# Cluster attention and two feed-forward layers on one core: preparation of the second and third pair of heads placed earlier, with a third buffer of queries and keys

## The chip, the cores and the metric

The kernel runs on one core of a Trainium2 chip, as one program. The metric is the device time of one execution in microseconds (us). Three executions of the kernel before gave 790.48, 790.6 and 793.39 us, with a median of 790.6 us.

## The reference

What is computed, cut to what matters (2 batches, 8 heads, 768 positions, 64 features a head, 16 centroids a head):

```python
def _attn_ref(q, k, v, centroids):
    q_n = q / (norm(q) + 1e-06); k_n = k / (norm(k) + 1e-06); c_n = centroids / (norm(centroids) + 1e-06)
    q_assign = np.argmax(np.einsum('bhsd,hcd->bhsc', q_n, c_n), axis=-1)
    k_assign = np.argmax(np.einsum('bhsd,hcd->bhsc', k_n, c_n), axis=-1)
    mask = q_assign[:, :, :, None] == k_assign[:, :, None, :]
    scores = np.where(mask, scale * q @ k.T, -1000000000.0)
    attn = softmax(scores)
    return attn @ v

x = attention output as [1536, 512]
h = np.maximum(x @ w_in, 0.0);  x = (h * h) @ w_out
h = x @ w_in2;                  out = (h * sigmoid(1.702 * h)) @ w_out2
```

A query sees only the keys of its own cluster. Inputs and result are float32, except that the weights come as float64 words.

## The kernel before

The work of attention goes by pairs of heads: eight pairs `p` (four a batch), two heads a pair. Scores are computed tile by tile: `scores(s)` is 128 queries of one head against all 768 keys, 96 tiles in all, and the two heads of a pair alternate, so that twelve tiles make a pair. A tile goes through `scores` (TensorE, L517 and L520, four matmuls into `ps_s`), `peak` (VectorE, L526, the row's extreme), `exponents` (ScalarE, L534), `turn` (TensorE, L542, twelve transposes for two tiles), `keep` (copies out of PSUM by VectorE and ScalarE, L550), and after six tiles `values` (TensorE, L560). There are two `ps_s` buffers, so that the matmuls of a tile wait for the exponentials of the tile two before. All other PSUM tiles (`ps_aff`, `ps_back`, `ps_oh`, `ps_p`, `ps_v`, `ps_r`) share four banks.

Before its first tile, a pair is prepared by `prep(p)`:

- `load` brings queries and keys (`raw_q`, `raw_k`) by the SP queue, L266. `q_high`, `k_high` (L357, L347) round them on ScalarE, `q_low`, `k_low` (L362, L352) subtract on GpSimd (POOL), each with a DMA that doubles the rounded half.
- `square` (L371) squares queries and keys, on ScalarE (L369) for the first two pairs and on POOL from the third on. `aff` (L378, L381) multiplies queries and keys by the centroids and sums the squares, in two halves of 384 positions; `aff_out` (L387) copies this to `cst`. These are the "products" below.
- `back` (L395) transposes `cst`, `back_out` (L405) copies it to `ar`; `root` (L409, POOL) and `inv_norm` (L415, L416, VectorE) make inverse norms, `scale` (L428, POOL), `most` (L436, VectorE), `less` (L439, POOL), `first`, `least`, `one_hot` (L443, L447, L454, VectorE) find the nearest centroid as a one-hot row.
- `mask` (L461) transposes the one-hot rows, `mask_out` copies them out of PSUM (L470 and L472 for the first pair, L477 for the others), and for the later pairs four DMAs (L482) put them below the queries and keys, where they enter L520 as 16 more rows of the contraction.

The order is written out by hand. Every step has a key, a number; all steps of the kernel are sorted by it, and each engine carries its own out strictly in that order. The tables FIRST (first pair), SECOND (second) and PAIR (all others) hold the keys of `prep`, counted from 12 times the pair; GROUP holds those of two tiles, two key units apart, from -1 on. So `aff` of the second pair, with -60.03 in SECOND, has key -48.03, and that of the third pair, with -15.15 in PAIR, has key 24 - 15.15 = 8.85. After the last pair the two feed-forward layers follow, matmuls of 128x512 (L656, L695), the weights converted by VectorE, ScalarE and POOL beside them (L191 to L213).

Of the kernel before, what the change touches and what calls it, by code (L numbers as in the profile page):

```python
# [8 lines left out]
F32 = mybir.dt.float32  # L9
# [7 lines left out]
P = 128  # L17
# [15 lines left out]
PAIR = dict(  # L33
    load_q=-20.601, load_k=-20.501, load_v=-5.2, square=(-16.9, -16.5),
    aff=(-15.15, -15.1), aff_out=(-14.95, -14.8), back=(-13.15, -13.1), back_out=(-12.95, -12.8),
    k_high=(-13.4, -6.9), k_low=(-12.95, -6.3), q_high=(-12.6, -10.7), q_low=(-12.2, -8.9),
    root=-12.7, inv_norm=-9.95, scale=-9.9, most=-8.98, less=-8.95, first=-6.98,
    least=-6.95, one_hot=-6.0, mask=(-5.15, -5.1), mask_out=(-4.95, -4.8),
)
# [5 lines left out]
FIRST = dict(  # L45
    load_v=-46.0, centres=-51.127, windows=-51.026, warm=(-51.2, -51.02, -48.752),
    square=(-49.995, -49.985), q_high=(-49.99, -49.98), k_high=(-48.1, -49.97),
    q_low=(-49.9, -49.8), k_low=(-47.95, -49.7),
    aff=(-49.195, -49.095), aff_out=(-49.145, -49.045), back=(-48.995, -48.895), back_out=(-48.95, -48.85),
    root=(-48.8, -48.7), inv_norm=-48.6, scale=-48.5, most=-48.4, less=-48.3, first=-48.117, least=-48.1,  # L50
    one_hot=-48.0, mask=(-47.9, -47.7), mask_out=(-47.859, -47.659, -47.559, -47.459), table=-48.107,
)
SECOND = dict(
    load_q=-62.0, load_k=-62.0, load_v=-1.143, square=(-60.05, -60.04), aff=(-60.03, -60.02), aff_out=(-59.44, -59.43),
    back=(-12.6, -12.59), back_out=(-12.5, -12.4), root=-12.35, inv_norm=-10.2, scale=-10.15, most=-8.25,
    less=-8.2, first=-6.98, least=-6.97, one_hot=-5.9, mask=(-3.15, -3.1), mask_out=(-2.95, -2.8),
    q_high=(-11.3, -5.4), q_low=(-10.1, -5.3), k_high=(-4.9, -3.4), k_low=(-4.8, -3.3),
)


# [5 lines left out]
def cluster_attention_then_two_ffns(  # L66
# [17 lines left out]
    nc = tc.nc  # L84
    B, H, D, S = q_t.shape
# [16 lines left out]
    scale = 1.0 / float(D) ** 0.5  # L102
# [6 lines left out]
    ROOM = {F32R: 96 * KB, F32: 110 * KB}  # L109
# [51 lines left out]
    g_at = [14 * KB + 6 * KB * m for m in range(MF)]  # L161
    g_t = [view(a, [NC, CH]) for a in g_at]
    tmp, o_p = Places(4 * KB, 10 * KB), Places(0, g_at[0])
    words_at = (0, 10 * KB)
    places = Places(g_at[0], g_at[15])


    def weight(layer, which, m):
# [7 lines left out]
    def w_stages(layer, which, m, place):  # L176
# [35 lines left out]
        def low():  # L212
            nc.gpsimd.tensor_tensor(out=halves[:, 1, :], in0=x[0].bitcast(F32), in1=halves[:, 0, :].bitcast(F32),  # L213
                                    op=ALU.subtract)

        return load, [magnitude, clamp, shift, join_low, join_high, high, low]


    with tc.manual_schedule():
        with ExitStack() as actx:  # L220
# [7 lines left out]
            one = places  # L228
# [5 lines left out]

            def early():

                for nm in ("raw_q", "raw_k", "sq"):
                    for _ in range(2):
                        places.tile([P, S], F32, tag=nm, bufs=2)
                places.tile([P, S], F32, tag="cst")  # L240
                places.tile([P, NT, P], F32, tag="ar")
                places.tile([P, NT, 4, C], F32, tag="aff")

            early()
            KQ = D + C
            x_s, k1_s, q2_s, k2_s = [], [], [], []
# [10 lines left out]
            def load(p, nm):  # L257
                b, hp = PAIRS[p]
                heads = slice(2 * hp, 2 * hp + 2)
                if nm == "v":  # L260
                    t = two.tile([P, 2, NT, D], F32, tag="v", name="raw_v")
                    src = v[b, :, heads]
                else:
                    t = one.tile([P, S], F32, tag="raw_" + nm, name="raw_" + nm, bufs=2)
                    src = (q_t if nm == "q" else k_t)[b, heads].rearrange("h d s -> (h d) s")
                (nc.scalar if p == 0 and nm == "q" else nc.sync).dma_start(out=t, in_=src)  # L266
                raw[p, nm] = t

            cr = one.tile([P, D], F32, name="cr")
            nc.sync.dma_start(out=cr, in_=centroids)  # L270
            load(0, "q")
            load(0, "k")
            half = one.tile([P, NT, 2, 2], F32, name="half")
            nc.vector.memset(half, 0.5)
# [56 lines left out]
            def at(key, f, *args):  # L331
                events.append((key, len(events), lambda: f(*args)))
# [5 lines left out]
            def prep(p):  # L338
# [45 lines left out]
                def aff_out(u):  # L384
                    if u == 0:
                        h["cst"] = one.tile([P, S], F32, tag="cst", name="cst")
                    nc.scalar.copy(  # L387
                        out=h["cst"][:, u * HALF:(u + 1) * HALF], in_=h["aff", u][:, :HALF])

                USED = 6 * C + 2  # L390
# [91 lines left out]
                            nc.sync.dma_start(out=dst[D:D + C].bitcast(F32), in_=m[r * C:(r + 1) * C].bitcast(F32))  # L482

                def put(name, f, *args):
                    when = (FIRST, SECOND, PAIR)[min(p, 2)]
                    w = when[name]
                    start = NQ * p
                    if isinstance(w, tuple):
                        for x, key in enumerate(w):
                            at(start + key, f, x)  # L490
                    else:
                        at(start + w, f, *args)

                for nm in ("q", "k", "v") if p else ("v",):
                    put("load_" + nm, load, p, nm)
                for name, f in (("square", square), ("root", root), ("inv_norm", inv_norm), ("k_high", k_high), ("k_low", k_low),
                                ("q_high", q_high), ("q_low", q_low), ("aff", aff), ("aff_out", aff_out), ("back", back),
                                ("back_out", back_out), ("scale", scale_rows), ("most", most), ("less", less),
                                ("first", first), ("least", least), ("one_hot", one_hot), ("mask", mask),
                                ("mask_out", mask_out)):  # L500
                    put(name, f)
# [103 lines left out]
            for k in range(NG // 2):  # L605
# [4 lines left out]
                for b in range(3):  # L610
                    at(begin + GROUP["turn"][b], turn, k, b)
                    when = GROUP["keep"][b]
                    at(begin + (when if b < 2 else when[k % 2 == 0]), keep, k, b)
            for n in range(NH):
                when, begin = (LAST, 0.0) if n == NH - 1 else (HALVES, ORIGIN + 6 * n)
# [208 lines left out]
```

## Time and profile before

| what | value |
|---|---|
| median of three runs | 790.6 us (790.48 to 793.39) |
| the profiled execution's own time | 790.69 us |
| its span, first to last instruction | 788.9 us |
| what lies around the span | 1.79 us |
| mean granted TensorE clock | 0.993 |
| PE busy | 775.4 us, 98% of the span |
| VectorE (DVE) / ScalarE (ACT) / POOL busy | 457.6 / 418.2 / 203.3 us |
| chain that ended last, by engine | PE 88%, DVE 6%, ACT 3%, POOL 1%, issue 1% |
| chain, largest lines | L656 32%, L695 28%, L560 8%, L542 7%, L517 5%, L520 4% |

The busy rows say how long an engine had an instruction in it; the chain says which engine's work set the end, followed back from the last instruction. The span in 40 slices shows PE at nine tenths or more in all but the first two slices and the last, and a granted clock below nine tenths of full speed in one, the second. In the rows of the trace a start is in us from the span's start, and a bracket tells the idle time ahead of an instruction and who ended it.

### The profile page before, as it was taken

The numbers are of one execution on the slowest core, as the hardware profiler recorded it, in microseconds if no ns is written. First come the engines' busy times: TensorE is split into PE (matmuls) and PEld (weight loads), VectorE is DVE, ScalarE is ACT, GpSimd is POOL, SyncE is SP. The second block draws the span as 40 slices with busy tenths as digits, with TensorE's granted clock in tenths as the row PEclk, the third lists the DMA queues.
The fourth block names the chain that finished last, engine by engine and source line by source line (L and its number), as shares of the span: only waits on it lengthen the run. The fifth ranks groups of instructions, "written<-read, shape, count | busy, mean of one in ns | idle before, by whom it ended". The sixth has DMA issues, their size and how long they took to land.

```text
span 788.9 us, 10653 instructions
## 1 busy us (share of the span) xinstructions
PE 775.4 (98%) x3947; PEld 610.5 (77%) x3947; DVE 457.6 (58%) x813; ACT 418.2 (53%) x775; POOL 203.3 (26%) x158
## 2 busy tenths in 40 slices
PE   7899999999999999999999999999999999999998
PEld 5766767767776788888887888888888888788886
DVE  6657877868877444444477644445654557742222
ACT  6776887887876466666643433343333334432222
POOL 2564654654601122212122011101211112200000
PEclk9799999999999999999999999999999999999999
DMA  4232222222120122232233022101212112210002
GB/s 141 69 85 69 81 66 76 81 67 76 41 84 28 59 99 91 99 102 86 81 107 107 27 70 64 54 0 60 102 53 81 54 62 99 81 54 0 1 1 106
DMA packets 18195, 54.52 MB, mean 69 GB/s; under 512 B 2720, under 2 KB 2976, under 8 KB 18144
## 3 DMA queue, kind: packets, MB, share of 16 engines
q1 hardware_dynamic: 17856, 53.32, 21.4%
q8 instruction: 31, 0.51, 0.3%
q10 hardware_dynamic: 288, 0.52, 0.2%
q14 instruction: 20, 0.16, 0.1%
HBM read 43.02 MB, written 3.15 MB: 59 GB/s over the span
## 4 chain that ended last, share of the span: by engine, by line
PE 88%; DVE 6%; ACT 3%; issue 1%; POOL 1%; DMA 0%; ACTq 0%; DVEq 0%; POOLq 0%
PE bank L656 32%; PE bank L695 28%; PE ps_v L560 8%; PE ps_p L542 7%; PE ps_s L517 5%; PE ps_s L520 4%; PE ps_h L656 1%; DVE arena L683 1%; ACT arena L534 1%; PE ps_aff L378 1%; DVE arena L526 1%; PE ps_r L577 1%; DVE arena L206 1%; DVE arena L194 1%; DVE arena L202 1%
## 5 line engine op out<-in xcount | busy, mean ns | idle before, releaser
L695 PE MATMUL bank<-arena 128*128 128x512 f32 x1152 | 262.3, 389 | 0.6 <-DVE arena L683 0.6
L695 PEld LDWEIGHTS bank<-arena 128*128 128x128 f32 x1152 | 215.9, 188 | 46.7 <-DVE arena L683 2.0
L656 PE MATMUL bank<-arena 128*128 128x512 f32 x1104 | 250.6, 389 | 0.0
L656 PEld LDWEIGHTS bank<-arena 128*128 128x128 f32 x1104 | 207.2, 188 | 43.0
L213 POOL TENSOR_TENSOR arena<-arena,arena 128x512 fp32r<-128x512 f32 x64 | 82.7, 1292 | 368.0 <-ACT arena L210 307.6
L683 DVE TENSOR_TENSOR arena<-arena,arena 128x512 fp32r<-128x512 f32 x96 | 74.8, 781 | 106.4 <-ACT arena L679 105.1
L526 DVE TENSOR_SCALAR_CACHE_REDUCE arena<-ps_s 128x768 bf16<-128x768 f32 x96 | 91.7, 956 | 42.8 <-PE ps_s L520 35.1
L679 ACT CAST arena<-arena 128x512 fp32r<-128x512 f32 x96 | 59.1, 619 | 105.0 <-PE bank L695 105.0
L534 ACT ACTIVATE arena<-ps_s,arena 128x768 f32<-128x768 f32 x96 | 86.9, 906 | 38.9 <-DVE arena L526 38.5
L194 DVE TENSOR_SCALAR arena<-arena 128x512 f32<-128x512 f32 x64 | 38.4, 599 | 73.7 <-ACT arena L191 73.7
L210 ACT CAST arena<-arena 128x512 fp32r<-128x512 f32 x64 | 39.6, 618 | 64.9 <-DVE arena L206 64.9
L542 PE MATMUL ps_p<-arena 128*128 128x128 f32 x576 | 73.1, 278 | 0.0
L560 PE MATMUL ps_v<-arena 128*64 128x384 f32 x384 | 72.6, 501 | 0.0
L665 ACT ACTIVATE arena<-bank 128x512 f32<-128x512 f32 x48 | 28.7, 598 | 79.0 <-PE bank L656 79.0
L542 PEld LDWEIGHTS ps_p<-arena 128*128 128x128 f32 x576 | 67.9, 144 | 2.3 <-issue 0.6
L672 DVE TENSOR_TENSOR arena<-bank,arena 128x512 f32<-128x512 f32 x48 | 33.1, 690 | 58.0 <-ACT arena L665 58.0
L517 PE MATMUL ps_s<-arena 128*128 128x384 f32 x192 | 55.5, 370 | 4.1 <-ACT arena L534 3.9
L520 PE MATMUL ps_s<-arena 80*128 80x384 f32 x192 | 50.5, 344 | 0.6 <-ACT arena L472 0.5
L517 PEld LDWEIGHTS ps_s<-arena 128*128 128x128 f32 x192 | 31.8, 192 | 20.9 <-ACT arena L534 9.3
L550 DVE COPY arena<-ps_p 128x512 f32<-128x512 f32 x72 | 47.0, 677 | 0.8 <-PE ps_p L542 0.8
L202 DVE SCALAR_TENSOR_TENSOR arena<-arena 128x512 int32<-128x512 int32 x64 | 45.3, 708 | 2.0
L206 DVE SCALAR_TENSOR_TENSOR arena<-arena 128x512 int32<-128x512 int32 x64 | 44.2, 691 | 1.9
(93 smaller groups left out, 636.3 us busy)
## 6 DMA issues: line engine op xcount, KB each, us to landing
arena<-in_w_dram SPq DMA_DIRECT2D x64, 512.0 KB, 3.2
arena<-arena SPq DMA_DIRECT2D x32, 192.0 KB, 2.5
arena<-in_k_t_dram SPq DMA_DIRECT2D x8, 384.0 KB, 3.7
arena<-in_v_dram SPq DMA_DIRECT2D x8, 384.0 KB, 3.3
out_dram<-arena SPq DMA_DIRECT2D x11, 256.0 KB, 2.1
arena<-in_q_t_dram SPq DMA_DIRECT2D x7, 384.0 KB, 3.3
arena<-arena SPq DMA_DIRECT2D x28, 48.0 KB, 2.1
arena<-in_q_t_dram ACTq DMA_DIRECT2D x1, 384.0 KB, 3.5
```

The lines of the kernel that those rows point to most:

```text
L202: nc.vector.scalar_tensor_tensor(out=x[0], in0=words[:, :, 0], scalar=29, in1=x[0], op0=ALU.logical_shift_right, op1=ALU.bitwise_or)
L213: nc.gpsimd.tensor_tensor(out=halves[:, 1, :], in0=x[0].bitcast(F32), in1=halves[:, 0, :].bitcast(F32), op=ALU.subtract)
L517: nc.tensor.matmul(ps[:, n, :HALF], lhsT=x_s[i][:, t * P:(t + 1) * P], rhs=k1_s[i][:, n * HALF:(n + 1) * HALF], start=True, stop=False)
L520: nc.tensor.matmul(ps[:, n, :HALF], lhsT=q2_s[i][:, t * P:(t + 1) * P], rhs=k2_s[i][:, n * HALF:(n + 1) * HALF], start=False, stop=True)
L526: nc.vector.tensor_scalar(out=unused, in0=s_t[g][:, :, :HALF], scalar1=-scale, scalar2=None, op0=ALU.mult, op1=ALU.min, accum_out=m_t[g])
L534: nc.scalar.activation(out=p_t[g].rearrange("p (n f) -> p n f", n=2), in_=s_t.pop(g)[:, :, :HALF], func=AF.Exp, bias=m_t.pop(g), scale=sca ...
L542: nc.tensor.transpose(ps[:, x * P:(x + 1) * P], p_t[2 * k + j][:, t * P:(t + 1) * P], ident)
L560: nc.tensor.matmul(pv_t[n][j * D:(j + 1) * D, :HALF], lhsT=raw[n // 2, "v"][:, j, t, :], rhs=pt_t[n, j][:, t, :], start=(t == 0), stop=(t ...
L656: nc.tensor.matmul(ps, lhsT=w[:, a, kk * P:(kk + 1) * P], rhs=xf[:, b, kk, c * CH:(c + 1) * CH], start=(n == 0), stop=(n == 3 * KD - 1))
L679: nc.scalar.copy(out=half_of(m, c)[:, 0, :], in_=g_t[m][:, c, :])
L683: nc.vector.tensor_tensor(out=t[:, 1, :], in0=g_t[m][:, c, :], in1=t[:, 0, :].bitcast(F32), op=ALU.subtract)
L695: nc.tensor.matmul(ps, lhsT=lhsT, rhs=rhs, start=(m == 0 and e == 0), stop=(m == MF - 1 and e == 2))
```

## The change

It gives the third pair a table of its own, THIRD, and new keys to some steps of the second and third pair:

- Second pair: `aff_out` and `back` move between the first pair's `aff` and its first scores (keys -47.95 and -47.6; the first masks have -47.9 and -47.7). `back_out` and `root` keep their places behind the first pair's `mask_out`. `first` and `least` move behind the `peak` of the tiles 6 and 7 (tiles are counted from 0). The roundings of the second head move a little earlier.
- Third pair: queries and keys are loaded ahead of the first values' load, its squares come first on POOL after the first pair's `q_low`, `aff` stands behind the scores of tiles 0 and 1 (keys 0.85 and 0.9), `aff_out` goes from ScalarE to VectorE, `back` stands ahead of the scores of tile 10 (keys 8.9 and 8.92), `back_out` follows.
- `raw_q` and `raw_k` have three buffers in place of two; the memory of attention grows by 6 KB, to the end of its arena.

```diff
-    load_q=-62.0, load_k=-62.0, load_v=-1.143, square=(-60.05, -60.04), aff=(-60.03, -60.02), aff_out=(-59.44, -59.43),
-    back=(-12.6, -12.59), back_out=(-12.5, -12.4), root=-12.35, inv_norm=-10.2, scale=-10.15, most=-8.25,
-    less=-8.2, first=-6.98, least=-6.97, one_hot=-5.9, mask=(-3.15, -3.1), mask_out=(-2.95, -2.8),
-    q_high=(-11.3, -5.4), q_low=(-10.1, -5.3), k_high=(-4.9, -3.4), k_low=(-4.8, -3.3),
+    load_q=-62.0, load_k=-62.0, load_v=-1.143, square=(-60.05, -60.04), aff=(-60.03, -60.02), aff_out=(-59.95, -59.94),
+    back=(-59.6, -59.59), back_out=(-59.44, -59.43), root=-59.35, inv_norm=-10.2, scale=-10.15, most=-8.25,
+    less=-8.2, first=-6.2, least=-6.15, one_hot=-5.9, mask=(-3.15, -3.1), mask_out=(-2.95, -2.8),
+    q_high=(-11.3, -6.18), q_low=(-10.1, -6.1), k_high=(-5.45, -4.75), k_low=(-5.4, -4.7),
+)
+THIRD = dict(
+    PAIR, load_q=-71.9, load_k=-71.89, square=(-71.4, -71.39), aff=(-23.15, -23.1), aff_out=(-22.95, -22.9),
+    back=(-15.1, -15.08), back_out=(-14.75, -14.7),
 )
...
-    places = Places(g_at[0], g_at[15])
+    places = Places(g_at[0], ROOM[F32])
...
-                for nm in ("raw_q", "raw_k", "sq"):
-                    for _ in range(2):
-                        places.tile([P, S], F32, tag=nm, bufs=2)
+                for nm, n in (("raw_q", 3), ("raw_k", 3), ("sq", 2)):
+                    for _ in range(n):
+                        places.tile([P, S], F32, tag=nm, bufs=n)
...
-                    t = one.tile([P, S], F32, tag="raw_" + nm, name="raw_" + nm, bufs=2)
+                    t = one.tile([P, S], F32, tag="raw_" + nm, name="raw_" + nm, bufs=3)
...
-                    nc.scalar.copy(
+                    (nc.vector.tensor_copy if p == 2 else nc.scalar.copy)(
                         out=h["cst"][:, u * HALF:(u + 1) * HALF], in_=h["aff", u][:, :HALF])
...
-                    when = (FIRST, SECOND, PAIR)[min(p, 2)]
+                    when = (FIRST, SECOND, THIRD, PAIR)[min(p, 3)]
```

In the lists below, the lines of the changed kernel are four higher than those of the kernel before.

TensorE from the first masks (`ps_oh`) to the first transposes of exponentials (`ps_p`), first as before, then as changed:

```order
L461 MATMUL ps_oh<-arena_58 128x128 x6
L517 MATMUL ps_s<-arena_58 128x384 x2
L520 MATMUL ps_s<-arena_58 128x384 x2
L517 MATMUL ps_s<-arena_58 128x384 x2
L520 MATMUL ps_s<-arena_58 128x384 x2
L395 MATMUL ps_back<-arena_59 128x98 x6
L517 MATMUL ps_s<-arena_58 128x384 x2
```

```order
L465 MATMUL ps_oh<-arena_58 128x128 x6
L399 MATMUL ps_back<-arena_59 128x98 x6
L521 MATMUL ps_s<-arena_58 128x384 x2
L524 MATMUL ps_s<-arena_58 128x384 x2
L521 MATMUL ps_s<-arena_58 128x384 x2
L524 MATMUL ps_s<-arena_58 128x384 x2
L382 MATMUL ps_aff<-arena_59 32x384 x2
L385 MATMUL ps_aff<-arena_59 32x384 x2
L382 MATMUL ps_aff<-arena_59 32x384 x2
L385 MATMUL ps_aff<-arena_59 32x384 x2
L521 MATMUL ps_s<-arena_58 128x384 x2
```

The six transposes of the second pair went ahead of the scores of tiles 0 and 1, and the eight products of the third pair came in behind them.

POOL from the first pair's `q_low` on, as before and as changed (`arena` is the memory that holds all tiles; 128x768 are squares, 128x24 is `root`):

```order
L362 TENSOR_TENSOR arena_58<-arena_59,arena_58 64x768
L409 TENSOR_TENSOR arena_59<-arena_59 128x24
L428 TENSOR_TENSOR arena_59<-arena_59 128x384
L362 TENSOR_TENSOR arena_58<-arena_59,arena_58 64x768
L439 TENSOR_TENSOR arena_59<-arena_59 128x384
L571 COPY arena_59<-arena_59 128x384
L362 TENSOR_TENSOR arena_58<-arena_59,arena_58 64x768
L371 TENSOR_TENSOR arena_59<-arena_59 128x768
```

```order
L366 TENSOR_TENSOR arena_58<-arena_59,arena_58 64x768
L375 TENSOR_TENSOR arena_59<-arena_59 128x768 x2
L413 TENSOR_TENSOR arena_59<-arena_59 128x24
L432 TENSOR_TENSOR arena_59<-arena_59 128x384
L366 TENSOR_TENSOR arena_58<-arena_59,arena_58 64x768
L443 TENSOR_TENSOR arena_59<-arena_59 128x384
L366 TENSOR_TENSOR arena_58<-arena_59,arena_58 64x768
```

Both squares of the third pair went ahead of the second pair's `root`.

VectorE around the tiles 4 to 7, as before and as changed (128x768 is `peak`, 128x4x128 a copy of transposed exponentials):

```order
L550 COPY arena_59<-ps_p 128x4x128 x2
L443 SCALAR_TENSOR_TENSOR arena_59<-arena_59 128x384
L447 TENSOR_REDUCE arena_59<-arena_59 128x24
L526 TENSOR_SCALAR arena_59<-ps_s 128x768 x2
```

```order
L554 COPY arena_59<-ps_p 128x4x128 x2
L530 TENSOR_SCALAR arena_59<-ps_s 128x768 x2
L447 SCALAR_TENSOR_TENSOR arena_59<-arena_59 128x384
L451 TENSOR_REDUCE arena_59<-arena_59 128x24
```

The two `peak` went ahead of `first` and `least`.

## Rows read from the trace of the kernel before

**Rows 1.** The page, busy time of PE, share of the span and instructions.

```profile
PE 775.4 (98%) x3947; PEld 610.5 (77%) x3947; DVE 457.6 (58%) x813; ACT 418.2 (53%) x775; POOL 203.3 (26%) x158
```

**Rows 2.** Busy time by stretch: us, each engine (instructions), PEclk, DMA share, GB/s.

```profile
20.00:30.00 10.00, 8.96 (x44) 8.37 (x44) 5.51 (x13) 7.17 (x16) 6.96 (x4) 0.69 0.31 100
30.00:40.00 10.00, 8.14 (x44) 6.20 (x44) 8.26 (x18) 7.55 (x16) 4.83 (x5) 0.83 0.18 41
...
80.00:100.00 20.00, 20.00 (x133) 15.00 (x133) 17.13 (x34) 16.16 (x34) 15.09 (x10) 1.00 0.34 94
```

**Rows 3.** Timeline of the first tiles: start, us, engine, line, what.

```profile
13.95 1.11 PE L381 MATMUL ps_aff<-arena 128*32 128x384 f32 x3
...
16.07 0.94 ACT L472 CAST arena<-ps_oh 16x384 fp32r<-16x384 f32 x2 [2.54 <-DVE arena L470]
16.59 0.62 PE L520 MATMUL ps_s<-arena 80*128 80x384 f32 x2 [0.47 <-ACT arena L472]
...
17.64 0.96 DVE L526 TENSOR_SCALAR_CACHE_REDUCE arena<-ps_s 128x768 bf16<-128x768 f32 x1
...
18.13 0.86 ACT L387 COPY arena<-ps_aff 128x384 f32<-128x384 f32 x2
...
19.18 0.84 ACT L405 COPY arena<-ps_back 128x294 f32<-128x294 f32 x2 [0.18 <-PE ps_back L395]
...
19.91 0.91 ACT L534 ACTIVATE arena<-ps_s,arena 128x768 f32<-128x768 f32 x1
...
20.96 1.01 PE L517 MATMUL ps_s<-arena 128*128 128x384 f32 x2 [1.39 <-ACT arena L534]
```

**Rows 4.** Timeline, PE: scores of tiles 4 and 6.

```profile
26.10 0.62 PE L517 MATMUL ps_s<-arena 128*128 128x384 f32 x2
...
29.31 0.62 PE L517 MATMUL ps_s<-arena 128*128 128x384 f32 x2
```

**Rows 5.** Busy time by stretch, around the two falls of the clock.

```profile
18.00:19.00 1.00, 0.64 (x5) 0.29 (x3) 0.87 (x3) 0.97 (x3) 0.00 (x0) 1.00 0.00 0
19.00:20.00 1.00, 0.57 (x5) 0.29 (x3) 0.70 (x2) 0.80 (x3) 0.00 (x0) 0.67 0.00 0
...
20.90:25.90 5.00, 4.94 (x19) 4.85 (x20) 2.87 (x7) 2.86 (x7) 3.87 (x2) 0.50 0.45 130
...
36.10:38.80 2.70, 2.70 (x16) 2.33 (x16) 1.69 (x5) 2.65 (x6) 2.39 (x2) 0.55 0.34 76
```

**Rows 6.** Timeline, tile 6: copies and peak on DVE, last scores on PE.

```profile
29.68 1.28 DVE L550 COPY arena<-ps_p 128x512 f32<-128x512 f32 x2
29.77 0.51 PE L520 MATMUL ps_s<-arena 80*128 80x384 f32 x2
...
31.92 0.95 DVE L526 TENSOR_SCALAR_CACHE_REDUCE arena<-ps_s 128x768 bf16<-128x768 f32 x1
```

**Rows 7.** Timeline: third pair's products, tile 10, its transposes.

```profile
40.97 0.52 PE L378 MATMUL ps_aff<-arena 128*32 128x384 f32 x2
...
41.42 1.46 POOL L371 TENSOR_TENSOR arena<-arena 128x768 f32<-128x768 f32 x1
42.93 0.83 PE L381 MATMUL ps_aff<-arena 128*32 128x384 f32 x2 [1.11 <-POOL arena L371]
...
44.35 0.52 PE L378 MATMUL ps_aff<-arena 128*32 128x384 f32 x2
...
45.13 0.62 PE L517 MATMUL ps_s<-arena 128*128 128x384 f32 x2
...
49.48 0.72 PE L395 MATMUL ps_back<-arena 98*128 98x98 f32 x6
```

**Rows 8.** Timeline, SP queue and POOL: first values' load, second pair's root.

```profile
12.58 0.58 SPq L266 DMA_DIRECT2D arena<-in_v_dram  x1
...
20.14 4.19 POOL L409 TENSOR_TENSOR arena<-arena 128x24 f32<-128x24 f32 x1 [12.39 <-issue]
```

**Rows 9.** Line L266, loads of queries, keys and values.

```profile
DMA to landing us min/median/max: 3.1/3.5/6.1
```

**Rows 10.** Chain that ended last, around 234 us: start, us, what.

```profile
234.54 0.57 ACT arena L191
```

## Prediction

> **What bounds the kernel now.** I read the page's busy times first: PE is busy 775.4 of 788.9 us [rows 1], so at most some 13 us of the span are free of matmuls. The table by stretches tells where: from 44 us on PE has hardly a gap (20.00 of 20.00 us between 80 and 100 at full clock [rows 2]), while between 20 and 40 it is busy for 8.96 and 8.14 us of ten, at a granted clock of 0.69 and 0.83 [rows 2]. What the first 45 us lose, the end is late by, because behind them PE is never short of work; and only what shortens those 45 us can pay. There the timeline says what PE waits for: tile 2 waits for the first exponentials, since scores have two buffers [rows 3]; the third pair's products wait 1.11 us for a square on POOL [rows 7]; and between 20.9 and 25.9 PE works at clock 0.50, the lower level, 1.2 GHz [rows 5].
>
> The change moves work out of the crowded 41 to 50 us into gaps before 21 us, and takes steps of the second pair out of ScalarE's and VectorE's way. Tiles are counted from 0. My yardstick is the start of tile 12, the first of the second pair. In both orders PE has by then done the same work, and what comes later is moved as a whole. The sum is made against the profiled execution's 790.69 us (span 788.9 and 1.79 around it), 0.1 above the median, which is neglected.
>
> **Step 1, first exponentials.** Before, ScalarE ends the first masks' copies at 17.16 + 0.95 = 18.11, then copies the second pair's products (18.13, 0.86), waits for PE's transposes, copies these (19.18, 0.84) and starts the first exponential at 19.91 [rows 3], though its peak, started at 17.64 for 0.96, was long there. Changed, the products' copies fall into ScalarE's idle 2.54 us ahead of 16.07 (the products end at 13.95 + 1.11 = 15.06 [rows 3], the second copy by about 15.5), and the transposes follow at once, to about 16.4. So only the 0.84 stand between: 18.13 + 0.84 = 18.97, which is **0.94 earlier**, and tile 2 starts at 20.96 - 0.94 = 20.02. The price is that tile 0's scores stand behind the transposes. Their second half waited until 16.59 for a mask copy anyway [rows 3]; pushed by 0.4 at most, they are still done when VectorE turns to their peak at 17.64. I cost it at nothing; if that cover is gone, 0.4.
>
> **Step 2, products of the third pair.** Before, their first half holds PE from 40.97 to 42.93 + 0.83 = 43.76, the wait for POOL's square included, the second from 44.35 to 45.13 [rows 7]: 2.79 + 0.78 = 3.57 us on PE's path. Changed, two halves of 0.78 run from about 18.4, behind tile 1, to 20.0, just as tile 2 may start. They need squares. SP issues those loads where the first values' load stood, 12.58, the keys 0.58 later; with 3.5 us to landing [rows 8, 9] they are there at 16.1 and 16.7. POOL is idle since 20.14 - 12.39 = 7.75 [rows 8] and takes 1.46 for each square [rows 7]: done by 16.1 + 2.92 = 19.0, in the middle of the first half, which may push the second to 20.2. The products' copies go to VectorE, which otherwise waits for tile 2's scores. The third pair's transposes, 0.72 at 49.48 [rows 7], only change sides of tiles 10 and 11, both ahead of my yardstick: nothing. **3.5 gained.**
>
> **Step 3, the clock.** From tile 2 (20.96) to tile 4 (26.10) take 5.14 us, the next two 29.31 - 26.10 = 3.21 at full clock [rows 3, 4]: 1.93 lost to the lower level. The second fall has 2.70 us of busy PE at 0.55 [rows 5], 2.70 x 0.45 = 1.21 lost; before the change POOL's square would have hidden that, with the square gone it counts. The clock falls within 19 to 20 us, and PE had been busy for only 0.64 of the microsecond ahead [rows 5]; that is where the transposes moved to and the eight products now stand. The second fall, at 36, comes behind the late tiles of step 4, which move together. I take both falls as gone: **3.1**. That is the least certain term: bounds 0 and 3.1.
>
> Of the Trainium skill, the page "TensorE: Matmul & The Clock Gate" (section "HAM oscillation — how this bites in real kernels") puts the fall down to one long wait of PE, its next section ("A second HAM failure mode: psum-queue depth-cycling") to frequent short idling between groups. By the first, filling short gaps would not hold the clock and the gain would be 3.8; by the second it is 6.9. The trace speaks for the second: a mean clock of 0.67 between 19 and 20 us is full speed for a third of it, so it fell near 19.3, and PE's longest wait there, 1.39 until 20.96, began only at 19.57 [rows 3, 5].
>
> **Step 4, peaks of tiles 6 and 7.** Tile 6's scores end at 29.77 + 0.51 = 30.28 and VectorE ends two copies at 29.68 + 1.28 = 30.96, but the peak starts at 31.92, behind `first` and `least` [rows 6]. These now come after: **0.96**.
>
> **Step 5, what is given back.** The products' end at 20.2 holds tile 2 by 0.2. Root starts behind the squares and the transposes' copies, at 19.0 in place of 20.14, and still takes 4.19 [rows 8]: done at 23.2. Tile 3 starts behind the second exponential, near 21.0; its scores take 30.28 - 29.31 = 0.97 and its peak 0.95 [rows 4, 6], so VectorE is free at 22.9 and stands at `inv_norm`, with a copy and tile 4's peak queued behind: 0.3. Tiles 8 to 11 come faster than the copies free PSUM banks, the masks of the second pair may wait for one; and tile 12 needs four mask DMAs that were far ahead before. No row prices these two; between nothing and the 1.11 that PE waits for the square now [rows 7], I take 1.1, the row nearest to them. Together **1.6**.
>
> Sum: 0.94 + 3.5 + 3.1 + 0.96 - 1.6 = 6.9. 790.69 - 6.9 = **783.8 us**. Without step 5's losses it is 8.5, or 782.2; without any gain of the clock 3.8, or 786.9.
>
> About 0.5%, 4 us, is what a measurement of this kernel can tell from no change; so "faster" begins at 786.6.
>
> **Rivals.**
>
> *The clock falls all the same, once or twice.* PE still idles between tiles until values begin, so another low stretch of 3 us is possible. For it: tiles 4 to 9 have not enough matmuls for PE, now as before. Against: all groups stand closer together. It gives back 1.2 to 3.1: 785.0 to 786.9, with other small losses to 787.4.
>
> *Squares come late.* Every load shown lands after 3.1 to 6.1 us [rows 9]. If the keys land at 13.1 + 6.1 = 19.2, POOL ends the second square at 20.7, 1.7 later than above, and with it tile 2's scores and root: 785.5; both this and a low clock, 788.6.
>
> *Slower by the same POOL queue.* Root stands behind the squares, VectorE's queue behind root, tile 2 behind the products. Each microsecond that the loads come after 17.4 us (18.97 less a square) costs one. 6.9 are used up when keys land at about 24.3, some 11 us after issue; at 26 the time is 792.4. For it: three loads now go out within two microseconds where one did. Against: no load shown took more than 6.1 [rows 9].
>
> *The gain is handed back later.* Around 234 us the chain runs through the weights' conversion on ScalarE [rows 10]; were this tied to time and not to the order, PE would wait there for what it won: 790. Against: those steps have keys like all others, and their loads go out by program order.
>
> **How the numbers follow.** Forecast, 782.2 to 785.0: 0.62. Clock falls again: 0.18, of which 0.11 ends below 786.6. Late squares: 0.10, 0.04 of it below, the rest with a lower clock. Handed back: 0.06. Slower by POOL: 0.04. So faster by over 0.5%: 0.62 + 0.11 + 0.04 = 0.77. Slower: 0.04 and 0.01 for late squares with more mishap than priced, 0.05. The same: 0.18. The range is 782.0, the sum without losses and 0.2 for the fastest run shown against the profiled one, to 787.4, the clock's worst case; outside lie the rest of the late squares, the handing back and the slower rival, less than 0.2.
>
> **What would show it.** Step 1: the first exponential at about 19.0, tile 2's scores at 20.0. Step 2: squares on POOL between 16 and 18.5, eight products between 18.4 and 20, no wait of products for POOL at 42. Step 3: granted clock 1.00 in every stretch of the first 45 us. Step 4: tile 6's peak straight behind two copies. Step 5: VectorE's L419 waiting for POOL near 23; tile 12 at about 43 in place of 49.96. It is wrong if tile 2 starts after 20.6, if the clock stays low for more than 3 us, or if tile 12 is early but the end is not.

## The result and the profile after

Four runs of the changed kernel gave 783.63 to 784.08 us, median **783.81**; four of the kernel before, 790.48 to 793.39, median 791.85. The ratio is 0.9901 with a 95% interval of 0.9884 to 0.9917: 8.0 us or 1.0% faster, beyond the half per cent that the prediction takes as the least that can be told from no change. The kernel before scatters by itself: of 57 executions timed beside the experiments 34 took 790.1 to 791.6 us and 23 took 792.3 to 793.5, so that the median 791.85 lies between two groups, and against the 790.69 us from which the forecast was reckoned the gain is 6.9. The profiled executions have spans of 788.9 and 781.9 us, 7.0 apart. The forecast was 783.8, in a range of 782.0 to 787.4.

The table of busy time by stretches, which answers to [rows 2], has in the changed kernel:

```profile
20.00:30.00 10.00, 9.13 (x60) 7.80 (x59) 8.74 (x19) 8.02 (x16) 7.41 (x5) 1.00 0.09 20
30.00:40.00 10.00, 8.93 (x61) 6.66 (x60) 7.31 (x16) 8.26 (x18) 5.03 (x4) 1.00 0.30 67
...
80.00:100.00 20.00, 20.00 (x139) 13.80 (x136) 16.16 (x32) 14.27 (x29) 9.69 (x8) 1.00 0.34 90
```

The granted clock is 1.00 where it was 0.69 and 0.83, and PE is busy for 9.13 us at that clock where 8.96 were partly at the lower level. Later nothing is different: PE was and is full.

To see where the time came from, I took the start of every second tile. The timeline of the changed kernel, PE, for the tiles 2, 4, 6, 8, 10, 12 and 20 (the L517 rows of [rows 3, 4, 7] are the tiles 2, 4, 6 and 10 before):

```profile
20.34 0.62 PE L521 MATMUL ps_s<-arena 128*128 128x384 f32 x2
...
23.39 0.62 PE L521 MATMUL ps_s<-arena 128*128 128x384 f32 x2
...
26.80 0.59 PE L521 MATMUL ps_s<-arena 128*128 128x384 f32 x2
...
30.49 0.62 PE L521 MATMUL ps_s<-arena 128*128 128x384 f32 x2
...
37.96 0.60 PE L521 MATMUL ps_s<-arena 128*128 128x384 f32 x2
...
42.30 0.62 PE L521 MATMUL ps_s<-arena 128*128 128x384 f32 x2
...
61.32 0.57 PE L521 MATMUL ps_s<-arena 128*128 128x384 f32 x2
```

The tiles 8, 12 and 20 of the kernel before, whose rows were not shown:

```profile
34.02 0.61 PE L517 MATMUL ps_s<-arena 128*128 128x384 f32 x2 [1.06 <-ACT arena L534]
...
49.99 0.60 PE L517 MATMUL ps_s<-arena 128*128 128x384 f32 x2
...
68.53 0.56 PE L517 MATMUL ps_s<-arena 128*128 128x384 f32 x2
```

Subtracting row from row (the changed profile's first steps came 0.13 us earlier, the second pair's last products at 13.82 in place of 13.95, which I take off the first line):

| stretch | before | changed | won | what ended there |
|---|---|---|---|---|
| to tile 2 | 20.96 | 20.34 | 0.49 | first exponentials; products of the third pair |
| tile 2 to 4 | 5.14 | 3.05 | 2.09 | lower clock gone |
| tile 4 to 6 | 3.21 | 3.41 | -0.20 | |
| tile 6 to 8 | 4.71 | 3.69 | 1.02 | peaks ahead of `first` and `least` |
| tile 8 to 12 | 15.97 | 11.81 | 4.16 | products and POOL's square gone, lower clock gone |
| tile 12 to 20 | 18.54 | 19.02 | -0.48 | given back, most of it at tile 19 |

The sum is 7.08, with the 0.13 of the start 7.21; the spans differ by 7.0. What was won by tile 20 reached the end but for 0.2.

### The profile page after: what moved, and what is told of

Same layout as the page of the kernel before. It is cut to its first block, busy times and chain, and to the rows that moved or that the text cites. A ratio compares the mean times of both kernels' runs of the same rounds, so it can differ in the third digit from the quotient of the medians.

```text
span 781.9 us, 10655 instructions
## 1 busy us (share of the span) xinstructions
PE 771.3 (99%) x3947; PEld 606.8 (78%) x3947; DVE 459.8 (59%) x815; ACT 417.4 (53%) x773; POOL 203.5 (26%) x158
## 4 chain that ended last, share of the span: by engine, by line
PE 88%; DVE 6%; ACT 3%; issue 1%; DMA 0%; POOL 0%; ACTq 0%; DVEq 0%; POOLq 0%
PE bank L660 32%; PE bank L699 28%; PE ps_v L564 8%; PE ps_p L546 7%; PE ps_s L521 4%; PE ps_s L524 4%; PE ps_h L660 1%; ACT arena L538 1%; DVE arena L687 1%; PE ps_aff L382 1%; DVE arena L530 1%; DVE arena L210 1%; DVE arena L198 1%; PE ps_r L581 1%; DVE arena L206 1%
## 5 line engine op out<-in xcount | busy, mean ns | idle before, releaser
L546 PE MATMUL ps_p<-arena 128*128 128x128 f32 x576 | 70.8, 272 | 0.0
L546 PEld LDWEIGHTS ps_p<-arena 128*128 128x128 f32 x576 | 65.7, 141 | 2.3 <-issue 0.6
```

The costliest lines, as they stand in the source:

```text
L546: nc.tensor.transpose(ps[:, x * P:(x + 1) * P], p_t[2 * k + j][:, t * P:(t + 1) * P], ident)
```

## Experiments

Six kernels undo or turn a piece of the change, two tried the clock by itself, and two went further than the change. A run's mean granted clock tells how long the lower level lasted: 3 us at half speed lower the mean over 789 us by 0.5 x 3 / 789 = 0.002. I give times by that mean. The changed kernel was timed once, beside the result; the kernel before was timed again beside every group of experiments, with medians of 791.03 to 791.45 and lowest times of 790.13 to 790.25. So a few tenths between an experiment and 783.81 say little unless a trace shows them too. The traces begin up to 0.6 us apart; where that matters, I count from the second pair's last products (L385), which start at 13.82 in the changed kernel.

### Step 1 undone (e1): the transposes back behind the first scores

```diff
-    load_q=-62.0, load_k=-62.0, load_v=-1.143, square=(-60.05, -60.04), aff=(-60.03, -60.02), aff_out=(-59.95, -59.94),
-    back=(-59.6, -59.59), back_out=(-59.44, -59.43), root=-59.35, inv_norm=-10.2, scale=-10.15, most=-8.25,
+    load_q=-62.0, load_k=-62.0, load_v=-1.143, square=(-60.05, -60.04), aff=(-60.03, -60.02), aff_out=(-59.44, -59.43),
+    back=(-12.6, -12.59), back_out=(-12.5, -12.4), root=-12.35, inv_norm=-10.2, scale=-10.15, most=-8.25,
```

> The changed kernel with step 1 undone: the second pair's products are copied, and transposed, behind the first scores again; the third pair's products stay where the change put them. Theory (step 1 frees ScalarE): the first exponential at 19.8, tile 2 about 0.9 us later than 20.34, root 1.2 later with VectorE behind it; 785.0 at full clock, 786.5 if the clock falls near 19 us. Rival (the transposes' place does nothing, the third pair's products and the clock do it all): 783.8, within 0.3.

Measured: 784.56 to 784.64 us in three runs with clock 1.000, 785.93 to 786.07 in three with 0.998. The timeline, ScalarE and PE:

```profile
18.62 0.86 ACT L391 COPY arena<-ps_aff 128x384 f32<-128x384 f32 x2
...
19.15 0.85 PE L399 MATMUL ps_back<-arena 98*128 98x98 f32 x6 [0.36 <-ACT arena L391]
...
19.66 0.79 ACT L409 COPY arena<-ps_back 128x294 f32<-128x294 f32 x2 [0.18 <-PE ps_back L399]
...
20.34 0.91 ACT L538 ACTIVATE arena<-ps_s,arena 128x768 f32<-128x768 f32 x1
...
21.39 0.62 PE L521 MATMUL ps_s<-arena 128*128 128x384 f32 x2
```

The copies stand between the masks and the first exponential again, and tile 2 is late: counted from the products (14.43 here), the first exponential comes 1.1 us later than in the changed kernel, tile 2 0.4 us. At full clock the step is worth 0.8 us; in half of the runs its undoing also brought one low stretch, for 1.4 more.

### Step 2 undone (e2): the third pair by the old table

```diff
-                    when = (FIRST, SECOND, THIRD, PAIR)[min(p, 3)]
+                    when = (FIRST, SECOND, PAIR, PAIR)[min(p, 3)]
```

(The products' copies go back to ScalarE with it.)

> The changed kernel with step 2 undone: the third pair goes by the table of the later pairs (loads, squares, products, transposes as before), step 1, the order of the peaks and the third buffer stay. Theory (products and POOL's square leave PE's path, 3.5 us): 787.3 at full clock, to 789 if the gap left before tile 2 lets the clock fall; a wait of some 1 us for POOL's square near 40 us comes back. Rival (the clock is what paid): within 1 us of 783.8 as long as the clock stays at full.

Measured: 788.05 us in the one run with clock 1.000, 789.70 with 0.998, 790.76 with 0.995, 790.97 to 791.35 in seven with 0.996, 792.04 and 792.15 with 0.994; the median of twelve is 791.09. So the step pays 4.2 us at full clock, by a single execution of which there is no profile, and leaving it out brings the low stretches back: three more units of 0.002 cost 4.0 more. The profiled run (0.996), busy time by stretch around PE's first idle time:

```profile
19.00:20.00 1.00, 0.00 (x0) 0.00 (x0) 0.91 (x2) 1.00 (x3) 0.66 (x1) 1.00 0.05 16
20.00:21.00 1.00, 0.85 (x4) 0.65 (x4) 0.06 (x2) 1.00 (x5) 1.00 (x1) 1.00 0.00 0
...
22.00:23.00 1.00, 1.00 (x7) 1.00 (x6) 0.87 (x3) 0.84 (x2) 1.00 (x1) 0.54 0.09 22
23.00:24.00 1.00, 1.00 (x7) 1.00 (x6) 0.62 (x5) 0.39 (x3) 0.53 (x1) 0.50 0.91 194
```

and the wait for POOL's squares further on:

```profile
38.49 0.83 PE L385 MATMUL ps_aff<-arena 128*32 128x384 f32 x2 [0.29 <-POOL arena L375]
...
40.40 1.47 POOL L375 TENSOR_TENSOR arena<-arena 128x768 f32<-128x768 f32 x1
...
41.92 0.89 PE L385 MATMUL ps_aff<-arena 128*32 128x384 f32 x2 [2.59 <-POOL arena L375]
```

PE comes to these products 3.6 us earlier than in the kernel before (37.36 for 40.97), POOL's squares only 1.0 to 1.2 us: the wait is 0.29 + 2.59 us where it was 1.11 [rows 7]. Steps 1 and 4 win little while this wait stands: 791.09 us, beside 791.45 for the kernel before (ratio 0.9987, 0.9975 to 0.9999).

### Step 4 undone (e3): first and least ahead of the peaks

```diff
-    less=-8.2, first=-6.2, least=-6.15, one_hot=-5.9, mask=(-3.15, -3.1), mask_out=(-2.95, -2.8),
+    less=-8.2, first=-6.98, least=-6.97, one_hot=-5.9, mask=(-3.15, -3.1), mask_out=(-2.95, -2.8),
```

> The changed kernel with step 4 undone: first and least ahead of the peaks of tiles 6 and 7 again, all else as changed. Theory: tile 6's peak starts 1.1 us later and tile 8 with it, 0.96 of it reaches the end: 784.8. Rival (the masks need first and least by then, so that it only changes what is late): 783.8, within 0.3.

Measured: 784.64, 784.70 and 785.04 us at clock 1.000, 785.90 to 786.48 at 0.998. The theory's 784.8 stands at full clock: 1.0 us, on the mean of the three. VectorE's order in the trace is that of [rows 6] again:

```profile
27.55 1.28 DVE L554 COPY arena<-ps_p 128x512 f32<-128x512 f32 x2
...
28.74 0.55 DVE L447 SCALAR_TENSOR_TENSOR arena<-arena 128x384 f32<-128x384 f32 x1
...
29.32 0.55 DVE L451 TENSOR_REDUCE arena<-arena 128x24 f32<-128x384 f32 x1
...
29.79 0.95 DVE L530 TENSOR_SCALAR_CACHE_REDUCE arena<-ps_s 128x768 bf16<-128x768 f32 x1
```

VectorE is through with the copies at 28.83 and takes up the peak at 29.79, 0.96 later.

### Steps 1 and 4 undone together (e9)

> The changed kernel with steps 1 and 4 both undone: against the kernel before, only the third pair's moves (and the buffers) are left. Theory (the parts add up, as their undoing alone cost 0.8 and 0.9 at full clock): 785.5 at full clock, 787 with one fall of the clock, 1.4 each. Rival (they hide each other: VectorE late for tile 6 is no loss if ScalarE was late for tile 2): 784.7, as with either alone.

Measured: 784.89 to 784.93 us at 1.000, 785.11 at 0.999, 786.26 and 786.60 at 0.998. At full clock the two cost 1.1 us together, where they cost 0.8 and 1.0 alone: nearer to the rival than to the sum. They hide each other in good part. The third pair's moves alone already give 785.0 us, 6.0 below the 791.04 of the kernel before that was timed beside them.

### Late squares (e10): root first on POOL

```diff
-    PAIR, load_q=-71.9, load_k=-71.89, square=(-71.4, -71.39), aff=(-23.15, -23.1), aff_out=(-22.95, -22.9),
+    PAIR, load_q=-71.9, load_k=-71.89, square=(-71.3, -71.29), aff=(-23.15, -23.1), aff_out=(-22.95, -22.9),
```

> The changed kernel with POOL's order turned: the second pair's root first, the third pair's squares behind it. It prices late squares, the way in which the change could have been slower. Theory (tile 2's scores stand behind products that wait for the squares, one for one): squares end at 25.9 in place of 18.9, tile 2 at 26.8 in place of 20.34, 790.2 at full clock, and a clock that falls in PE's wait of 7 us, 791.5 to 793. Rival (tile 2 has slack): less than 3 us lost, below 787.

Measured: 792.33 us (791.88 to 792.96), ratio to before 1.0011 (1.0001 to 1.002), at mean clocks of 0.994 to 0.996: all of the gain is lost, the price of the low clock included.

```profile
19.36 4.19 POOL L413 TENSOR_TENSOR arena<-arena 128x24 f32<-128x24 f32 x1 [11.26 <-issue]
...
23.51 2.90 POOL L375 TENSOR_TENSOR arena<-arena 128x768 f32<-128x768 f32 x2
...
25.04 2.27 PE L385 MATMUL ps_aff<-arena 128*32 128x384 f32 x3 [5.59 <-POOL arena L375]
...
28.69 0.62 PE L521 MATMUL ps_s<-arena 128*128 128x384 f32 x2
```

Tile 2 starts at 28.69 in place of 20.34, behind the squares. Counted from the second pair's products (14.33 here), the squares end at 25.9 as expected; tile 2 comes 2.28 us behind them, where the changed kernel has 1.47 (20.34 - 18.87) and the expectation had 0.9. The clock had fallen in the wait, near 21.3, and stayed at 0.50 to 28.05, so that the products themselves ran at the lower level. So my slower rival was a real one in kind: it takes one pair of instructions in the wrong order on POOL.

### Two buffers again (e6)

```diff
-                for nm, n in (("raw_q", 3), ("raw_k", 3), ("sq", 2)):
+                for nm, n in (("raw_q", 2), ("raw_k", 2), ("sq", 2)):
```

(and `bufs=2` in `load`.)

> The changed kernel with two buffers of queries and keys as before. The queries' first buffer is last read at 8.6 us, the keys' at 14.8. Theory (squares wait for loads, tile 2 for squares): the keys' load is held until 14.8 on SP with the values' load behind it, lands near 18, POOL's second square ends at 19.5 in place of 18.87, tile 2 and root some 0.6 later; 784.4. Rival (the third buffer is needed): the loads stand until the squares of tile 0's pair are through and cost 2 us or more, 786. Other rival (no use at all): 783.8.

Measured: 784.49 us (784.35 to 784.65), all runs at clock 1.000. In the trace the keys' load goes out at 15.25 and lands after 3.1 us, at 18.35; the bracket of the second square names an instruction of PE that ended at about that time:

```profile
15.25 0.33 SPq L270 DMA_DIRECT2D arena<-in_k_t_dram  x1
...
18.53 1.47 POOL L375 TENSOR_TENSOR arena<-arena 128x768 f32<-128x768 f32 x1 [0.69 <-PE ps_s L524]
...
20.05 0.51 PE L385 MATMUL ps_aff<-arena 128*32 128x384 f32 x1 [0.76 <-POOL arena L375]
...
21.45 0.62 PE L521 MATMUL ps_s<-arena 128*128 128x384 f32 x2
```

Counted from the second pair's products (14.16 here), the squares end 0.8 us later than in the changed kernel and tile 2 starts 0.8 us later. The third buffer is worth 0.7 us, by way of load, square, products and tile 2. The larger part of the change needs no memory.

### The clock by itself (e4, e5): two tries that did not show it

The kernel before with idle matmuls in PE's gaps, first into PSUM tiles of their own:

```diff
...
+            for key, n in ((-47.6, 4), (-0.65, 3), (0.85, 7)):
+                at(key, fill, n)
```

> The kernel before with 14 idle matmuls of 128x384 put into PE's gaps: four between the first masks and the first scores, three ahead of the second pair's transposes, seven behind them. Nothing else moves: it tests the clock alone. Theory (short idling lets the clock fall): granted clock 1.00 from 18 to 26 us, tile 4 within 3.3 us of tile 2 in place of 5.14, and 1.5 to 2.0 us less than before at the end, about 789; a fall near 36 may remain and costs nothing there. Rival (the fall comes from longer waits, which stay): clock 0.50 after 20 us and the time of before or up to 0.5 more.

Measured: 792.96 us (790.64 to 793.84), slower than before by 0.12% (0 to 0.24%). The time against the kernel before is no test of the clock:

```profile
18.14 1.03 PE L309 MATMUL fill<-arena 128*128 128x384 f32 x4 [1.98 <-ACT arena L478]
...
18.97 0.84 PE L523 MATMUL ps_s<-arena 128*128 128x384 f32 x2
```

The first filler needed one of the four shared banks and waited 1.98 us, until a mask had been copied out; tile 0 stood behind it. The second try wrote into unused columns of tiles that are there anyway:

```diff
...
+                    if p == 1 and u == 1:
+                        fill(ps, 16)
...
```

> The clock alone, again, without a new PSUM tile: the kernel before, with idle matmuls of 128x128 into columns that nothing reads of tiles that are there anyway: ten behind the first masks, six ahead of the second pair's transposes, sixteen behind them. Theory (short idling lets the clock fall): clock 1.00 from 16 to 26 us, tile 4 within 3.4 us of tile 2, tile 2 at most 0.4 late, and 1.0 to 2.0 us less than before in the same call. Rival (the falls come from longer waits, which stay): clock 0.50 for some 3 us near 20 and the time of before, or up to 0.5 more.

Measured: 792.95 us (791.49 to 795.43). Here the copies waited for the filler, though they read other columns of the tile:

```profile
20.60 1.98 PE L308 MATMUL ps_back<-arena 128*128 128x128 f32 x16
...
22.62 0.40 ACT L413 COPY arena<-ps_back 128x294 f32<-128x294 f32 x1 [1.71 <-PE ps_back L308]
```

The clock stayed at 1.00 through the filled stretch and fell near 24.8, behind a new wait of 1.39 us (to 23.97). That fits filled gaps keeping the clock, but as the fall that did come stood behind one longer wait, the run does not tell short gaps from such a wait. Its price can be read from both kernels, as from the runs above, since each was timed at several mean clocks: the first took 790.64 and 791.00 us at 1.000, 791.88 to 792.62 at 0.998 and 793.30 to 793.84 at 0.995 and 0.996; the second, less clearly, 791.49 and 791.81, then 791.56 to 793.16, then 792.88 to 794.38 at 0.996.

### Two steps further (e7, e8)

The third pair's loads go ahead of the last doubled half of the first pair's keys; and then also the third pair's search for the nearest centroid goes behind the peaks, as the change did for the second pair:

```diff
-    PAIR, load_q=-71.9, load_k=-71.89, square=(-71.4, -71.39), aff=(-23.15, -23.1), aff_out=(-22.95, -22.9),
-    back=(-15.1, -15.08), back_out=(-14.75, -14.7),
+    PAIR, load_q=-72.2, load_k=-72.19, square=(-71.4, -71.39), aff=(-23.15, -23.1), aff_out=(-22.95, -22.9),
+    back=(-15.1, -15.08), back_out=(-14.75, -14.7), most=-8.2, less=-8.15, first=-6.2, least=-6.15, one_hot=-5.95,
```

The loads alone (e7, the first changed line without the second):

> The changed kernel with the third pair's loads one step earlier on SP, ahead of the last doubled half of the first pair's keys, which waits for ScalarE until 11.9 us. Theory (tile 2 waits for products, these for squares, these for loads): squares start when the second pair's products have read their buffers, 15.1 in place of 15.98, end at 18.0, tile 2 starts at 19.7 in place of 20.34; 783.2. Rival (loads now take the queues from the first pair's halves): tile 0 or 1 starts later, 784 or more.

Measured: 783.15 us (783.03 to 783.26).

```profile
15.11 3.01 POOL L375 TENSOR_TENSOR arena<-arena 128x768 f32<-128x768 f32 x2 [6.96 <-PE ps_aff L385]
...
16.38 0.60 PE L521 MATMUL ps_s<-arena 128*128 128x384 f32 x2
...
20.17 0.62 PE L521 MATMUL ps_s<-arena 128*128 128x384 f32 x2
```

Squares start at 15.11, and tile 2 at 20.17 with tile 0 at 16.38: 3.79 us behind tile 0 in place of 4.46 (20.34 - 15.88). Tile 0 itself is as far behind the second pair's products as in the changed kernel, so the rival did not come true.

Both (e8):

> The same early load, and the third pair's most, less, first, least and one_hot put behind the peaks they stood ahead of, as the change did for the second pair. In the changed kernel tile 17 waits 0.39 us for ScalarE at 57 us, behind a most that waits for POOL. Theory: another 0.4 to 0.5, 782.7. Rival (the one-hot rows, and with them the third pair's masks, come late): no gain over the early load alone, 783.2 or more.

Measured: **782.78 us** (782.69 to 782.91), ratio to before 0.9892 (0.9875 to 0.9908). It is the lowest of all. What the expectation calls tile 17 is tile 19, counted from 0 as everywhere here. In the changed kernel VectorE waited for POOL with the peaks of the tiles 16 and 17 behind it, and tile 19 came 1.37 us behind tile 18:

```profile
53.21 0.55 DVE L440 TENSOR_REDUCE arena<-arena 128x24 f32<-128x384 f32 x1 [0.47 <-POOL arena L432]
...
53.68 0.95 DVE L530 TENSOR_SCALAR_CACHE_REDUCE arena<-ps_s 128x768 bf16<-128x768 f32 x1
...
55.77 0.62 PE L521 MATMUL ps_s<-arena 128*128 128x384 f32 x2
...
57.14 0.62 PE L521 MATMUL ps_s<-arena 128*128 128x384 f32 x2 [0.39 <-ACT arena L538]
```

In the kernel before the same wait for POOL is there (0.48 us, at 60.42), and tile 19 comes 1.02 us behind tile 18. What is new is that tile 16's peak starts 2.36 us behind tile 16's scores in place of 1.90: the subtraction ahead of it (L600) took 2.12 us in place of 1.67, as the last section shows.

With both steps the tiles 18 and 19 follow each other without a gap:

```profile
55.38 0.62 PE L521 MATMUL ps_s<-arena 128*128 128x384 f32 x2
...
56.18 0.51 PE L521 MATMUL ps_s<-arena 128*128 128x384 f32 x2
```

## Why the prediction was right

The time came out to the tenth, and part of that was luck. The sum was made against one execution of 790.69 us of a kernel that takes from 790.1 to 793.5. At the yardstick, tile 12, the two profiles are 7.56 us apart (49.99 - 42.30 - 0.13) where the sum says 6.9, and behind it, where all was to be moved as a whole, 0.48 was given back by tile 20. Terms that were too small and losses that were too small made up for each other.

**What bounds it** stood: PE is close to full behind 44 us, and what the first tiles won arrived, but for these 0.48 and 0.2 more behind tile 20.

**Step 1**, forecast 0.94: the first exponential starts at 18.60, which is 1.18 won with the 0.13 of the start taken off, but tile 2 only at 20.34, since the third pair's products still held PE. The rows of the changed kernel:

```profile
15.98 2.89 POOL L375 TENSOR_TENSOR arena<-arena 128x768 f32<-128x768 f32 x2 [8.35 <-PE ps_back L399]
...
18.60 0.92 ACT L538 ACTIVATE arena<-ps_s,arena 128x768 f32<-128x768 f32 x1
...
18.83 4.19 POOL L413 TENSOR_TENSOR arena<-arena 128x24 f32<-128x24 f32 x1
...
18.93 0.14 PEld L385 LDWEIGHTS ps_aff<-arena 128*32 128x32 f32 x2 [0.67 <-POOL arena L375]
```

The bracket of the squares names PE, but the queries' load, issued at 12.46 and landing after 3.4 us, ended just ahead of them, and in e7 an earlier load let them start earlier. They end at 18.87, as worked out (19.0), and the products behind them hold tile 2 by some 0.7 us (it could have followed the first exponential by 1.05 us as before), not by the 0.2 of step 5; e7, with earlier squares, won that 0.7 back. Undone alone the step is worth 0.8.

**Step 2**, forecast 3.5: 4.2 at full clock (e2, one execution), with what these moves gave back under step 5 already taken off. The term took the wait for POOL at the 1.11 us of the profile; with the other steps made and the third pair as before, it is 2.88 in e2's trace, because PE comes 3.6 us earlier and POOL's squares only 1.0 to 1.2. How much of these 1.8 us more is in the 4.2 stays open, as that trace also has low stretches.

**Step 3**, forecast 3.1: both low stretches are gone. In the two profiles the tiles 2 to 4 won 2.09, for which 1.93 was forecast, and the tiles 8 to 12 won 4.16, which is about the products, the second stretch and the 0.66 of step 5 together: 3.57 + 1.21 - 0.66 = 4.12. That the clock and not another wait made up these shares was not measured by itself. One stretch of some 3 us costs 1.0 to 1.7 us in e1, e2, e3 and e9. What is left of the gain behind 4.2 for step 2 and 1.1 for steps 1 and 4 is 1.5 against 790.69 us and 2.7 against the median, two estimates from these times. In the kernel before, a longer time at the low clock often cost nothing: nine executions took 790.35 to 790.60 us at 0.998 and nine 790.13 to 790.58 at 0.995 and 0.996, which fits the prediction's reading that the wait for POOL's square hid the second stretch. Of the two sections of the Trainium skill's page ("TensorE: Matmul & The Clock Gate") that the prediction weighs, the one on frequent short idling fits better: in the profile before the clock fell near 19.3 us, and between 12 us and then no wait of PE was longer than 0.52. No run tests short gaps alone. The rival in which the clock falls all the same did not come true in any run of the changed kernel (0.999 to 1.000); with step 1 or 4 undone it did in half of them (e1, e3).

**Step 4**, forecast 0.96: 1.0 undone alone, and 1.02 between tile 6 and tile 8; but undone together steps 1 and 4 cost 1.1 (e9), less than the sum of both, which the prediction's sum left out.

**Step 5**, forecast 1.6 given back: VectorE did not wait for root, which ended at 23.02 (18.83 + 4.19), ahead of the end of the peak at 23.40. The masks and the third pair's transposes waited for banks and copies:

```profile
35.90 0.38 PE L465 MATMUL ps_oh<-arena 128*64 128x128 f32 x3 [0.32 <-ACT arena L554]
...
37.34 0.84 PE L399 MATMUL ps_back<-arena 98*128 98x98 f32 x6 [0.34 <-ACT arena L481]
```

0.66 of the 1.1; the mask DMAs held nothing. With the 0.7 at tile 2, the 0.20 between tile 4 and 6 and the 0.48 behind tile 12, most of it at tile 19, of which the prediction has nothing, some 2.0 was given back in all.

**Rivals.** Late squares and the slower one by POOL's queue were told rightly in kind: a square that ends 7 us late costs all, with the low clock that comes of it (e10), one that ends 0.8 us late 0.7 (e6). The loads landed in time, the keys 3.7 us after their issue; the last moment for them is 17.5 (18.97 less 1.46), not 17.4, which changes nothing. Nothing to speak of was handed back near 234 us: behind tile 20 it is 0.2 in all.

## What to carry to other kernels

Where one engine is full from some moment to the end, only the stretch ahead of that moment can pay, and nearly all that is won there arrives; so look for steps of later stages that fit into its gaps, and follow each of them back through every queue that it stands in, since one instruction in the wrong order on a side engine (a root ahead of two squares) gave the whole gain away, with the low clock that followed it. Take a wait's price not from the profile but from who would end last once the other steps are made. Time single steps by undoing them, and together as well: here two of them hid each other in part.

## What the runs showed of the hardware

- The clock can fall with a delay. In e2's profile PE stands idle through 19 to 20 us, is busy again behind it, and only at about 22.1 falls to the lower level (0.54 for 22 to 23), at which it then worked to 25.5. Whoever looks there for the cause where the clock falls looks at a busy engine; in e10 it fell within the wait, near 21.3.
- One execution of the same kernel has several low stretches, another none: e2 took 788.05 us at mean clock 1.000 and 792.1 at 0.994. The changed kernel's four runs lie within 0.45 us, those of the kernel before within 2.9: with the change the scatter was gone too.
- A subtraction on VectorE (L600, 128x384) took 2.12 us at 49.64 in the changed kernel, where the shortest of its kind took 0.548; POOL was at a subtraction until 51.35:

```profile
49.53 1.82 POOL L366 TENSOR_TENSOR arena<-arena,arena 64x768 fp32r<-64x768 f32 x1
...
49.64 2.12 DVE L600 TENSOR_TENSOR arena<-arena,arena 128x384 fp32r<-128x384 f32 x1
```

The Trainium skill, page "SBUF — State Buffer", section "Who interferes with whom", says that a VectorE instruction with two inputs in SBUF contends with a GpSimd instruction that reads SBUF. The trace agrees: the subtraction ends 0.41 us behind POOL's, as if it had waited 1.71 us and worked 0.41. The kernel before has the same, less long, as its subtraction met POOL's (56.73 to 58.55) later:

```profile
57.30 1.67 DVE L596 TENSOR_TENSOR arena<-arena,arena 128x384 fp32r<-128x384 f32 x1
```

It ends 0.42 us behind POOL's, and so does a `first` of the changed kernel, 0.97 us long at 30.39 in place of 0.55, with POOL busy until 30.94. The 0.45 us between 2.12 and 1.67 are what VectorE came later by at tile 16, as these rows have it; no run takes it away by itself.
